# Attention projections as pairs of 64-row matmuls, from the fourth batch on, in a kernel whose order a planner writes

## The chip, the cores and the metric

One core of one Trainium2 chip. The metric is the time of one execution on the device, in microseconds; the kernel before takes 316.47 us, the median of three runs (316.13 to 316.59). Its profiled execution has a span of 314.5 us, with TensorE's granted clock at 1.000.

## What is computed

Attention with random features (Performer), followed by an MLP with a hard-swish gate:

```
q, k, v: (8 batches, 8 heads, 576 tokens, 64); omega: (128 features, 64); fp32
phi(x) = exp(h - max(h)) / sqrt(128),  h = (x s) omega^T - |x s|^2 / 2,  s = 64^-0.25
kv = phi(k)^T v;  z = sum over tokens of phi(k)
attention = phi(q) kv / (phi(q) z + 1e-6)
x = attention as (4608 tokens, 512);  w_in: (512, 2048), w_out: (2048, 512)
h = x w_in;  out = (h * clip(h + 3, 0, 6) / 6) w_out
```

The contraction of the projections `x omega^T` is over the head dimension, 64, half of TensorE's 128 rows.

## The kernel before, in words

**Order.** The kernel doesn't write its instructions in a fixed order. It records its work as operations (`op`, line 86), each with its engine or a choice of engines, an assumed duration, a priority, what it reads and writes, and the PSUM banks that it needs. A list scheduler (`schedule`, line 138) then plays them through on assumed times: of the operations whose inputs are ready it takes the one with the lowest priority number on each engine, and gives out the eight PSUM banks of 128 x 512 fp32 (`ring`) as they come free. `slack` and `dslack` make an operation wait a little longer than its inputs are assumed to take, `spare` asks for so many more free banks than it takes. `emit` writes the result with semaphore waits, so each engine has one fixed queue. The table `NUDGE` (line 20) adds a small number to the priorities of named operations; it was found by a search. No assumed time appears on the chip: a wrong one only gives an order that waits.

**Attention, per batch** (`attention`, line 587). The 576 tokens of 8 heads are 72 chunks of 128 x 64, two side by side in one "double chunk": 18 double chunks. `kT` and `qT` hold them turned, so that the 64 dimensions of the one chunk are on partitions 0 to 63 and those of the other on 64 to 127. For batches 0 to 2 TensorE turns them (L468), from batch 3 on the DMA queues do.
- K (line 676 to 692): for each double chunk, one matmul of all 128 rows with `kT` as weights and `om`, 128 x 256, streaming (L681). `om` is omega transposed twice on the diagonal, with zeros elsewhere, so both chunks come out side by side, in half a PSUM bank; two double chunks fill one bank. ScalarE takes the exponential of a bank (L687), VectorE its maximum by chunk (L690), because the division by the maximum is put off to `v`.
- Q (`project`, line 694): `om[:, lh, :]` as weights, half of whose rows are zero, and up to four double chunks of `qT` streaming, 512 columns; once for lh = 0, once for lh = 1, each into a bank of its own (L698). ScalarE takes the exponential (L702).
- `pair` (line 780), for each two heads: reciprocal of the maxima, `v` scaled by it (L794 on GpSimd or VectorE, L796 on ScalarE), phi(k)^T v and z by L810 and L812, phi(q) times that by L838, and the division by L854.

**MLP, per block of 512 tokens.** `mm1` (line 891): 16 groups of four matmuls of 512 columns (L907), each evacuated by a relu on ScalarE (L913) and a product on VectorE (L915). The second product is done, after the first block, as a seven-product Strassen form (`products`, line 1009, matmuls L1041, sums of tokens on GpSimd L973, sums of results on VectorE L1057). Block b's MLP is recorded beside the attention of batch b + 1, so TensorE's queue is a mixture of both; at the start, while inputs load, fill matmuls (`idle_work`, L505) hold TensorE's clock up.

Of the kernel before, what the change touches and what calls it, by code (L numbers as in the profile page):

```python
# [9 lines left out]
AF = mybir.ActivationFunctionType  # L10
AX = mybir.AxisListType


URGENT = 0.5
FIT = 0.1
IDLE_UNTIL = 21.0
EV0 = (("ACT","DVE"), ("ACT","DVE"), ("POOL","DVE"), {"k": ("POOL", "ACT", "DVE"), "q": ("POOL", "ACT","DVE")})
# [1 line left out]

NUDGE = {  # L20
    ('Tevk0.00', 0): 0.0222, ('Tk0.10', 0): 0.0169, ('Tevk0.10', 0): 0.0216, ('Tk0.11', 0): 0.0313,
    ('Tevk0.11', 0): 0.0172, ('castq0.0A', 0): -0.0176, ('Tq0.1B', 0): -0.0037, ('Tk0.l', 0): 0.0668,
    ('Tevk0.l', 0): -0.1599, ('K0.0', 0): -0.1553, ('eK0.0', 0): -0.0153, ('K0.1', 0): 0.0442,
    ('eK0.1', 0): -0.0653, ('mx0.1', 0): -0.0395, ('eK0.2', 0): -0.042, ('K0.3', 0): 0.0328, ('K0.5', 0): -0.0067,
    ('K0.6', 0): -0.0736, ('eK0.6', 0): 0.0218, ('K0.7', 0): -0.0092, ('eK0.7', 0): 0.0218, ('K0.8', 0): 0.0351,
    ('eK0.8', 0): 0.0218, ('mx0.8', 0): -0.0031, ('kvz.0.0', 0): 0.0057, ('num.0.0A', 0): 0.0042,
    ('rec.0.0A', 0): -0.0049, ('div.0.0A', 0): 0.0356, ('num.0.0B', 0): 0.0126, ('kv.0.1', 0): -0.0134,
    ('num.0.1A', 0): 0.0126, ('rec.0.1A', 0): -0.009, ('Xev.0.1A', 0): 0.0018, ('num.0.1B', 0): -0.0007,
    ('cc.0.2', 0): -0.0088, ('num.0.2A', 0): 0.0126, ('vc.0.3', 0): -0.0114, ('vcc.0.3', 0): -0.0172,
    ('num.0.3A', 0): 0.0126, ('X.0.3B', 0): 0.0821, ('Xev.0.3B', 0): 0.0062, ('numL0', 0): -0.0033,  # L30
    ('divL0', 0): 0.0082, ('divL2', 0): 0.0082, ('k00.1', 0): 0.0095, ('kl.1', 0): -0.0088, ('ql0.1', 0): 0.0145,
    ('vl.1', 0): -0.119, ('v10.1', 0): -0.0099, ('Tevq1.2', 0): 0.0463, ('Tq1.4', 0): 0.0008,
    ('mx1.7', 0): -0.0202, ('mx1.8', 0): 0.0033, ('Q1.0', 1): 0.0073, ('eQ1.0', 1): 0.0199, ('Q1.1', 0): 0.0184,
    ('Q1.1', 1): -0.0218, ('eQ1.1', 1): 0.0077, ('eQ1.2', 1): -0.007, ('vcl.1', 1): -0.0035, ('vc.1.0', 0): 0.0089,
    ('kv.1.0', 0): 0.0071, ('kvz.1.0', 0): -0.0003, ('rec.1.0A', 0): 0.0024, ('div.1.0A', 0): 0.0054,
    ('div.1.0B', 0): 0.0054, ('vc.1.1', 0): 0.0087, ('num.1.1A', 0): -0.002, ('div.1.1A', 0): 0.0054,
    ('div.1.1B', 0): 0.0054, ('Xev.1.1', 0): -0.0002, ('kv.1.2', 0): -0.0042, ('rec.1.2A', 0): -0.0101,
    ('div.1.2A', 0): 0.0075, ('div.1.2B', 0): 0.0054, ('X.1.2', 0): 0.0047, ('rec.1.3A', 0): -0.0016,
    ('div.1.3A', 0): 0.0054, ('div.1.3B', 0): 0.0054, ('mm1.0A.0p', 2): 0.0169, ('mm1.0A.2p', 1): 0.003,
    ('mm1.0A.2p', 2): 0.026, ('mm1.0A.4p', 2): 0.0282, ('mm1.0A.4', 0): 0.0113, ('relu.0A.4', 0): 0.1116,  # L40
    ('mm1.0A.6', 0): -0.0758, ('relu.0A.6', 0): -0.0575, ('mm1.0A.8', 0): -0.0075, ('g.0A.8', 0): -0.037,
    ('g.0A.10', 0): 0.0321, ('relu.0A.12', 0): 0.0317, ('mm1.0A.14', 0): 0.0222, ('relu.0B.12', 0): -0.0169,
    ('k10.2', 0): -0.0002, ('ql0.2', 0): 0.0037, ('K2.5', 0): -0.0042, ('mx2.5', 0): -0.1483, ('K2.7', 0): -0.0504,
    ('K2.8', 0): -0.1148, ('mm2.0.0', 3): -0.0049, ('mm2.0.0', 6): 0.0051, ('mm2.0.1', 2): 0.0111,
    ('mm2.0.1', 5): -0.0042, ('relu.1.7', 0): 0.0128, ('g.1.7', 0): -0.0389, ('g.1.8', 0): 0.0106,
    ('mm2.0.2', 0): -0.0003, ('relu.1.9', 0): 0.0261, ('mm1.1.11', 0): -0.0435, ('mm1.1.12', 0): 0.0488,
    ('k10.3', 0): -0.0369, ('kl.3', 0): 0.0052, ('q00.3', 0): -0.0024, ('q10.3', 0): 0.0694, ('ql0.3', 0): -0.0408,
    ('ql1.3', 0): -0.013, ('kv.3.2', 0): 0.1102, ('kvz.3.3', 0): 0.0243, ('g.2.1', 0): -0.019,
    ('mm2.1.3', 1): 0.0578,
}  # L50


# [24 lines left out]
class Prog:  # L77
# [8 lines left out]
    def op(self, eng, occ, emit, prio, reads=(), writes=(), alloc=(), lat=0.2, group=None, inc=1, name="", slack=0.0, dslack=0.0, issue=0.5, spare=0, packet=46.0):  # L86
        o = Op()
        o.engs = (eng,) if isinstance(eng, str) else tuple(eng)
        o.eng = None
        o.emit, o.occ, o.lat, o.prio, o.name = emit, occ, lat, prio, name  # L90
        o.alloc = list(alloc)
        o.group, o.inc, o.slack, o.dslack, o.issue, o.spare, o.packet = group, inc, slack, dslack, issue, spare, packet
        o.seq = len(self.ops)
        deps = {}
        virts = []
        for kx in reads:
            for d in self.w.get(kx, ()):
                deps[d] = True
            self.r.setdefault(kx, []).append(o)
            if isinstance(kx, Virt):  # L100
                virts.append(kx)
        for kx in writes:
            for d in self.r.get(kx, ()):
                if d is not o:
                    deps.setdefault(d, False)
            for d in self.w.get(kx, ()):
                deps.setdefault(d, False)
            self.w[kx] = [o]
            self.r[kx] = []
            if isinstance(kx, Virt):  # L110
                virts.append(kx)
        for vx in set(virts):
            vx.users.append(o)
            vx.left += 1
        o.virts = list(set(virts))
        o.deps = deps
        o.succ = []
        o.end = o.start = None
        o.emitted = None
        self.ops.append(o)  # L120
        return o
# [231 lines left out]
def _emit(nc, es, q, k, v, omega, w_in, w_out, out):  # L353
    B, H, S, D = q.shape
    M = omega.shape[0]
# [7 lines left out]
    NU = NCH // 4  # L363
# [3 lines left out]
    TU = [(0, 2), (2, 6), (6, 10), (10, 14), (14, 18)]  # L367
# [6 lines left out]
    alpha = float(D) ** -0.25  # L374
# [8 lines left out]
    K0, T0, V0, C0 = EV0  # L383
# [12 lines left out]
    vl = [sbt("vl%d" % u, [128, NP, D + 1], F32) for u in range(2)]  # L396
# [5 lines left out]
    kT = sbt("kT", [128, NDC, 128], BF16)  # L402
    qT = sbt("qT", [128, NDC, 128], BF16)
    qpT = [sbt("qpT", [128, NCH * 128], BF16)] * 2
    kp = [sbt("kp", [128, NCH, M], BF16)] * 2
    mx = [sbt("mx%d" % u, [128, NCH], F32) for u in range(2)]
    cc = [sbt("cc%d" % u, [128, NCH], F32) for u in range(2)]
    vc = [sbt("vc%d" % u, [128, 520], BF16) for u in range(2)]
# [30 lines left out]
    op = G.op  # L439

    def mmt(n):
        return 0.003 + n / 2400.0

    def actt(n):
        return 0.07 + n / 1200.0

    def dvet(n):
        return 0.07 + n / 960.0
# [138 lines left out]
    def attention(b):  # L587
# [80 lines left out]
        else:  # L668
            for t, cst, dst in (("k", KB[pb], kT), ("q", QB[pb], qT)):
                for i, (x0, x1) in enumerate(((0, 10), (10, 18))):  # L670
# [2 lines left out]
                       pos(4.5 * i) - 0.1, reads=rows_of(t, range(x0, x1)),  # L673
                       writes=[(t + "T", x) for x in range(x0, x1)], group="d%sT%d" % (t, i), inc=16,
                       lat=1.0, name="Tdma%s.%d.%d" % (t, b, i), issue=1.2, packet=24.0)
        for u in range(NU):
            vK = Virt(ring)

            def e_K(E, u=u, vK=vK):
                for i in range(2):  # L680
                    ins = E.matmul(ring.t[vK.slot][:, 256 * i:256 * i + 256], kT[:, 2 * u + i, :],  # L681
                                   om[:].rearrange("d t m -> d (t m)"), start=True, stop=True)
                return ins

            op("PE", 2 * mmt(256), e_K, pos(u) + 0.02, reads=[("kT", 2 * u), ("kT", 2 * u + 1)] + omk, writes=[vK],
               alloc=[vK], lat=0.25, slack=sl, dslack=2 * sl, spare=sp, name="K%d.%d" % (b, u))
            op("ACT", actt(512), lambda E, u=u, vK=vK: E.activation(  # L687
                kp[pb][:, 4 * u:4 * u + 4, :].rearrange("p c m -> p (c m)"), ring.t[vK.slot], AF.Exp, scale=alpha),
               pos(u) + 0.02, reads=[vK], writes=[("kp", 0, u)], name="eK%d.%d" % (b, u))
            op("DVE", dvet(512), lambda E, u=u: E.reduce_max(  # L690
                mx[pb][:, 4 * u:4 * u + 4], kp[pb][:, 4 * u:4 * u + 4, :], axis=AX.X),
               pos(u) + 0.03, reads=[("kp", 0, u)], writes=[("mx", pb, u)], name="mx%d.%d" % (b, u))
# [12 lines left out]

        qv = qpT[pb][:].rearrange("m (x l t) -> m x l t", l=2, t=128)
        for i, (d0, d1) in enumerate(TU):
            if i == 0 or b:
                project(str(i), list(range(d0, d1)), qT[:, d0:d1, :],
                        lambda lh, d0=d0, d1=d1: qv[:, d0:d1, lh, :], pos(2 * i) + 0.03 if b else LATE)  # L710
        if b == 0:
# [3 lines left out]
                    project("%d%s" % (m0 // 2, "AB"[s]), every(m0, m1, s), alts(qT, s, m0, m1),  # L715
                            lambda lh, s=s, m0=m0, m1=m1: qa[:, 2 * m0:2 * m1, s, lh, :], 0)
        op("DVE", 0.17, lambda E: E.reciprocal(cc[pb][:, 0:NP], mx[pb][:, 0:NP]), pos(0) + 0.04,
           reads=[("mx", pb, 0)], writes=[("cc", pb, "l")], name="ccl.%d" % b)
        for hh in range(2):
            p0 = 64 * hh  # L720
            op(EV_V if b else V0, {"POOL": 0.72, "DVE": dvet(260)}, lambda E, hh=hh, p0=p0: E.tensor_tensor(
# [58 lines left out]
    def pair(b, m, t):  # L780
# [25 lines left out]
        def e_kv(E):  # L806
# [4 lines left out]
                         start=(i == 0), stop=False)  # L811
            return E.matmul(o[:, 0:130], kp[pb][:, m, :], vcl[pb][:, m, :], start=False, stop=True)  # L812

        op("PE", 8 * 0.03 + 0.06, e_kv, t, reads=[("kp", 0, u) for u in us + [0]] +
           [("vc", u2, i) for i in range(2)] + [("vcl", pb, i) for i in range(2)],
           writes=[vkv], alloc=[vkv], lat=0.25, slack=sl, spare=sp, name="kv" + nm)
        op(EV_K if b else K0, both(130), evac(lambda: kvz[m][:], lambda: ring.t[vkv.slot][:, 0:130]), t, reads=[vkv],
# [405 lines left out]
```

The softmax here doesn't subtract the row's maximum and nothing guards it: scores larger than these inputs give would overflow.

## Time and profile before

| what | time, share or count |
|---|---|
| time, median of 3 | 316.47 us |
| span of the profiled execution | 314.5 us |
| VectorE, GpSimd, ScalarE busy | 74, 72, 64% of the span |
| mm1's matmuls (L907), 512 columns | 512 |
| Strassen products (L1041), 256 columns | 880 |
| K projections (L681), 256 columns | 144 |
| Q projections (L698), 512 or 256 columns | 80 |
| fill matmuls (L505) | 61 |

A row of the page reads: line, engine, operation, what it writes and reads, shapes and how many; then the time in which the engine was busy with them and the mean length of one in ns; then how long the engine sat idle just before them, and which engine's work ended that. TensorE's matmuls overlap in the pipeline and their ends are modelled, so the length of one record (379 ns for 512 columns) is not what it adds to the time; that is read from the starts of successive groups in the timeline.

### The profile page before, as it was taken

The page shows a single profiled execution, that of the slowest core. Times are in us where ns is not written, and L with a number is a line of the kernel's source. Part 1 is how long each engine was busy: PE and PEld are TensorE (multiplying, and loading weights), DVE is VectorE, ACT ScalarE, POOL GpSimd, SP SyncE. Part 2 cuts the span into 40 slices and gives each one's busy share as a digit, 9 for nine tenths or more (in the row PEclk, how much of TensorE's full clock was granted, in tenths as well). Part 3 has the DMA queues.
Part 4 walks back from the last instruction along what each step waited for, and adds up shares of the span by engine and source line. Part 5 has one row for each costly group of instructions (what it writes and reads, how often), then busy time and mean ns, then how long its engine had stood idle before and what let it go on. Part 6 is the DMA issues. An engine that isn't in the chain of part 4 may idle for free.

```text
span 314.5 us, 7018 instructions
## 1 busy us (share of the span) xinstructions
PE 307.1 (98%) x2662; PEld 214.2 (68%) x2662; DVE 233.8 (74%) x511; ACT 200.3 (64%) x465; POOL 227.1 (72%) x247
## 2 busy tenths in 40 slices
PE   8899999999999999999999999999999989999994
PEld 6689956656885688657855785668655954666684
DVE  4979998878799887697399767785879547556533
ACT  3987997899767957863299478842986026343300
POOL 2777253099879987599999896987577819868570
PEclk9999999999999999999999999999999999999999
DMA  8999989554996999099979993999205200300125
GB/s 244 286 202 210 235 133 230 171 67 42 173 216 75 127 257 204 2 127 219 194 161 126 237 186 84 122 240 223 76 15 104 85 9 0 134 2 2 67 85 117
DMA packets 83218, 43.15 MB, mean 137 GB/s; under 512 B 51057, under 2 KB 80881, under 8 KB 83185
## 3 DMA queue, kind: packets, MB, share of 16 engines
q1 hardware_dynamic: 55824, 29.60, 41.0%
q0 software_dynamic: 26576, 12.46, 32.2%
q10 hardware_dynamic: 784, 0.66, 0.7%
q8 instruction: 21, 0.34, 0.5%
q14 instruction: 13, 0.10, 0.1%
HBM read 36.73 MB, written 9.44 MB: 147 GB/s over the span
## 4 chain that ended last, share of the span: by engine, by line
PE 87%; DMA 6%; ACT 2%; DVE 2%; SPq 2%; issue 0%
PE p L907 35%; PE p L1041 31%; DMA v<-in_v_dram 6%; PE p L698 5%; PE p L681 4%; PE p L957 3%; PE p L838 3%; PE p L810 3%; PE p L468 2%; SPq L542 1%; ACT vc L796 1%; ACT kp L687 1%; PE p L932 1%; PE p L1107 1%; PE p L812 1%; DVE mx L690 0%
## 5 line engine op out<-in xcount | busy, mean ns | idle before, releaser
L913 ACT ACTIVATE tsb<-p 128x512 f16<-128x512 f32 x128 | 76.1, 604 | 54.7 <-PE p L907 53.9
L915 DVE SCALAR_TENSOR_TENSOR gT<-tsb,p 128x512 f16<-128x512 f16 x128 | 85.8, 683 | 28.0 <-ACT tsb L913 27.4
L907 PE MATMUL p<-xT,wi 128*128 128x512 bf16 x448 | 106.5, 379 | 0.0
L907 PEld LDWEIGHTS p<-xT,wi 128*128 128x128 bf16 x448 | 42.2, 98 | 42.0
L973 POOL TENSOR_TENSOR s<-gT 128x512 f16<-128x512 f16 x32 | 37.2, 1163 | 22.8 <-DVE gT L915 21.9
L687 ACT ACTIVATE kp<-p 128x512 bf16<-128x512 f32 x72 | 39.0, 611 | 22.5 <-PE p L681 22.5
L690 DVE TENSOR_REDUCE mx<-kp 128x4 f32<-128x512 bf16 x72 | 46.0, 667 | 8.3 <-ACT kp L687 8.3
L1041 PE MATMUL p<-wo,gT 128*128 128x256 f16 x368 | 45.2, 273 | 0.0
L702 ACT ACTIVATE qpT<-p 128x512 bf16<-128x512 f32 (+1 forms) x80 | 41.7, 577 | 1.9 <-PE p L698 1.7
L973 POOL TENSOR_TENSOR gT<-gT,s 128x512 f16<-128x512 f16 x32 | 36.9, 1153 | 6.1 <-PE p L1041 3.7
L1041 PEld LDWEIGHTS p<-wo,gT 128*128 128x128 f16 x368 | 35.8, 98 | 7.7
L973 POOL TENSOR_TENSOR s<-gT,s 128x512 f16<-128x512 f16 x32 | 37.0, 1158 | 4.1 <-DVE gT L915 2.7
L973 POOL TENSOR_TENSOR gT<-gT 128x512 f16<-128x512 f16 x32 | 36.9, 1152 | 2.5
L1041 PE MATMUL p<-t,gT 128*128 128x256 f16 x256 | 32.4, 273 | 0.8 <-DVE u L1057 0.8
L854 DVE TENSOR_TENSOR xb<-p,rec 128x384 bf16<-128x384 f32 (+1 forms) x64 | 28.6, 476 | 0.1
L1041 PEld LDWEIGHTS p<-t,gT 128*128 128x128 f16 x256 | 24.6, 98 | 5.9 <-DVE u L1057 1.1
L796 ACT ACTIVATE vc<-v,cc 128x64 bf16<-128x64 f32 x104 | 26.4, 362 | 1.2 <-DVE cc L788 1.1
L698 PE MATMUL p<-qT,om 128*128 128x512 bf16 (+1 forms) x80 | 24.4, 358 | 0.1
L794 POOL TENSOR_TENSOR vc<-v,cc 128x512 bf16<-128x512 f32 x17 | 17.8, 1045 | 8.4 <-DVE cc L788 6.2
L681 PE MATMUL p<-om,kT 128*128 128x256 bf16 x144 | 22.0, 274 | 0.0
L542 POOL DMA_DIRECT2D k<-in_k_dram x12 | 9.4, 786 | 16.4 <-PE p L907 15.5
L1057 DVE TENSOR_TENSOR u<-p 128x512 f32<-128x512 f32 x16 | 11.0, 688 | 12.3 <-PE p L1041 12.3
(94 smaller groups left out, 438.3 us busy)
## 6 DMA issues: line engine op xcount, KB each, us to landing
v<-in_v_dram SPq DMA_DIRECT2D x14, 512.0 KB, 7.1
out_dram<-osb SPq DMA_DIRECT2D x14, 512.0 KB, 3.7
wi<-in_moe_w_in_dram POOLq DMA_DIRECT2D x4, 512.0 KB, 9.3
k<-in_k_dram POOLq DMA_DIRECT2D x8, 256.0 KB, 4.7
k<-in_q_dram POOLq DMA_DIRECT2D x8, 256.0 KB, 7.0
wo<-in_moe_w_out_dram POOLq DMA_DIRECT2D x8, 256.0 KB, 11.3
kb<-in_k_dram POOLq DMA_DIRECT2D x6, 256.0 KB, 4.6
qb<-in_q_dram POOLq DMA_DIRECT2D x6, 256.0 KB, 6.8
```

The source lines that it names most:

```text
L681: ins = E.matmul(ring.t[vK.slot][:, 256 * i:256 * i + 256], kT[:, 2 * u + i, :], om[:].rearrange("d t m -> d (t m)"), start=True, stop=True)
L687: op("ACT", actt(512), lambda E, u=u, vK=vK: E.activation(kp[pb][:, 4 * u:4 * u + 4, :].rearrange("p c m -> p (c m)"), ring.t[vK.slot], AF ...
L690: op("DVE", dvet(512), lambda E, u=u: E.reduce_max(mx[pb][:, 4 * u:4 * u + 4], kp[pb][:, 4 * u:4 * u + 4, :], axis=AX.X), pos(u) + 0.03, r ...
L698: op("PE", mmt(n), lambda E, vQ=vQ, lh=lh: E.matmul(ring.t[vQ.slot][:, 0:n], om[:, lh, :], src, start=True, stop=True), p + 0.045 * lh, re ...
L702: op("ACT", actt(n), lambda E, vQ=vQ, lh=lh: E.activation(dst(lh), ring.t[vQ.slot][:, 0:n].rearrange("m (j t) -> m j t", t=128), AF.Exp, s ...
L796: ins = E.activation(vcm[:, i, 0:D], v32[:, m, i, :], AF.Copy, scale=cc[pb][:, c0 + i:c0 + i + 1])
L854: op("DVE", dvet(128 * n), lambda E: E.tensor_tensor(xv(i0, i1), psum()[:, :, :, 0:64], rbc, ALU.mult), t + 0.01, reads=[vn, ("rec", ru)], ...
L907: ins = E.matmul(ring.t[vh.slot], wi[:, c, 128 * f:128 * f + 128], xv[:, c, :], start=(c == 0), stop=(c == NJ - 1))
L913: op("ACT", actt(512), lambda E: E.activation(tsb[tu][:], ring.t[vh.slot], AF.Relu, bias=0.5, scale=1.0 / 6.0), t - 0.1, reads=[vh], write ...
L915: op("DVE", dvet(512), lambda E: E.scalar_tensor_tensor(gT[gu][:, f, :], tsb[tu][:], 1.0, ring.t[vh.slot], ALU.min, ALU.mult), t - 0.1, re ...
L973: op(engines, {"POOL": 0.05 + n / 490.0, "DVE": 0.07 + n / 1920.0}, lambda E: E.tensor_tensor(dst, x, y, ALU.subtract if minus else ALU.ad ...
L1041: ins = E.matmul(ring.t[v.slot][:, 256 * j:256 * j + 256], a[:, f, 128 * j:128 * j + 128], w[:, f, :], start=(first and f == 0 and j == 0) ...
```

## The change

From batch 3 on (`ROWS = 3`), K and Q of a range of double chunks are projected together by one operation on TensorE, `project_rows`. Each matmul uses only the 64 rows that hold its chunk: partitions 0 to 63 for the one, 64 to 127 for the other, with the matching half of `om`, so no product with zeros is left, and the two can run side by side in the two halves of the array. A range of four double chunks takes four banks at once (K and Q, each for both halves), the first range of two takes two banks. There are five such bursts in a batch. For K there are now twice as many matmuls, of 128 columns instead of 256. The planner counts such a burst as 0.22 us (`SWITCH`) plus the time of two full-width streams of its length. The exponentials and maxima are taken by half instead of by double chunk, with a step over the other half in what they write. The leftover tokens' keys get names of their own (`kpl`, `mxl`), so that the operations that need them depend on their burst alone.

The table `NUDGE` is replaced: many more entries, and larger ones (before up to 0.16, after up to 3.3), so that operations of the whole kernel, batches 0 to 2 and the MLP too, stand in another order and in part on another engine. TensorE's list has 59 fill matmuls instead of 61, and ScalarE's has 72 scalings of 64 elements (`vc`) instead of 104, GpSimd's 22 of 512 elements instead of 17.

```diff
+SWITCH = 0.22
+ROWS = 3
...
 NUDGE = {
...
-        for u in range(NU):
+        def project_rows(i, d0, d1):
+            n = d1 - d0
+            u = max(2 * i - 1, 0)
+            vs = [Virt(ring) for _ in range(2 if n == 2 else 4)]
+            def bank(w, lh):
+                c = 128 * n * w if n == 2 else 0
+                return vs[lh if n == 2 else 2 * w + lh], c
+            def out_of(w, lh):
+                vx, c = bank(w, lh)
+                return ring.t[vx.slot][:, c:c + 128 * n]
+            def e(E):
+                for x in range(n):
+                    for lh in range(2):
+                        E.matmul(out_of(0, lh)[:, 128 * x:128 * x + 128], kT[64 * lh:64 * lh + 64, d0 + x, :],
+                                 om[64 * lh:64 * lh + 64, lh, :], start=True, stop=True)
+                for lh in range(2):
+                    ins = E.matmul(out_of(1, lh), om[64 * lh:64 * lh + 64, lh, :],
+                                   qT[64 * lh:64 * lh + 64, d0:d1, :], start=True, stop=True)
+                return ins
+            op("PE", SWITCH + 2 * mmt(128 * n), e, pos(u) + 0.02,
+               reads=[(t + "T", x) for t in "kq" for x in range(d0, d1)] + omk, writes=vs, alloc=vs, lat=0.25,
+               slack=sl, dslack=2 * sl, spare=0, name="R%d.%d" % (b, i))
...
+        if b >= ROWS:
+            for i, (d0, d1) in enumerate(TU):
+                project_rows(i, d0, d1)
+        for u in range(NU if b < ROWS else 0):
...
-            if i == 0 or b:
+            if b < ROWS and (i == 0 or b):
                 project(str(i), list(range(d0, d1)), qT[:, d0:d1, :],
```

## The prediction

> **What bounds the kernel now.** I read the page's busy line, its forty slices and the chain first, then TensorE's own waits, then the timeline of TensorE in one steady stretch, because a busy TensorE need not be a full one.
>
> ```profile
> PE 307.1 (98%) x2662; PEld 214.2 (68%) x2662; DVE 233.8 (74%) x511; ACT 200.3 (64%) x465; POOL 227.1 (72%) x247
> PE   8899999999999999999999999999999989999994
> ...
> PE 87%; DMA 6%; ACT 2%; DVE 2%; SPq 2%; issue 0%
> ...
> L681 PE MATMUL p<-om,kT 128*128 128x256 bf16 x144 | 22.0, 274 | 0.0
> ```
>
> No other engine is over 74%, and the chain is 87% TensorE. All of TensorE's idle time that has a cause is in three single waits (columns: total us, times, longest us):
>
> ```profile
> PE p L505 <- DVE fill L500: 1.3, 1, 1.3
> PE p L810 <- DVE vcl L721: 0.9, 1, 0.9
> PE p L1041 <- DVE u L1057: 0.8, 1, 0.8
> ```
>
> The first two lie before 16 us. The timeline (start, us, group) then says whether the busy time is dense:
>
> ```profile
> 157.73 0.60 PE L681 MATMUL p<-om,kT 128*128 128x256 bf16 x4
> 158.17 4.48 PE L907 MATMUL p<-xT,wi 128*128 128x512 bf16 x20
> 162.49 0.60 PE L698 MATMUL p<-qT,om 128*128 128x256 bf16 x3
> 162.92 1.03 PE L907 MATMUL p<-xT,wi 128*128 128x512 bf16 x4
> 163.78 0.38 PE L698 MATMUL p<-qT,om 128*128 128x512 bf16 x1
> 164.00 0.42 PE L810 MATMUL p<-vc,kp 128*128 128x65 bf16 x8
> 164.26 0.22 PE L812 MATMUL p<-vcl,kp 128*128 128x130 bf16 x1
> ```
>
> Start to start, 20 matmuls of 512 columns take 162.49-158.17 = 4.32 us, 0.216 each; four of 256 take 0.44, 0.109 each; eight of 65, each with a weight load of its own, take 0.26, 0.033 each. That is one column per cycle at 2.4 GHz plus some 2 ns, with no pause between groups: the stream is full. From about 20 us to the last matmul near 310 us the time is the sum of these pitches, so what leaves TensorE's stream leaves the span, unless a new wait appears.
>
> **What the Trainium skill says.** "TensorEngine Tiling (Array Packing)", Key Properties: two 64-row tiles can load weights and multiply in parallel, and changing the tiling mode, not just the tile, drains TensorE. "TensorE: Matmul & The Clock Gate", Part 3, The mechanism: a weight load overlaps a running matmul of another row group, and two matmuls of different row groups start some 4 ns apart. The trace of before has only 128-row matmuls (every form reads 128*128), so it shows neither the pairing nor the drain. The first page's Gotcha 1: PSUM Pressure adds that concurrent row tiles need different PSUM banks; the new code gives the two halves of a pair different banks.
>
> **The change part by part.** (1) Removed, batches 3 to 7: 18 K matmuls of 256 columns per batch (L681, half of whose products are with the zero half of `om`), 18 x 0.109 = 1.96 us, and eight Q matmuls of 512 and two of 256 (L698), 8 x 0.216 + 2 x 0.109 = 1.95 us. Five batches: 5 x 3.91 = 19.5 us of the full stream.
>
> (2) Added: 36 K matmuls of 128 columns and the same ten Q matmuls per batch, all 64 rows high, so in pairs. K: 90 pairs in all. One matmul of 128 columns streams in 0.056 (the transposes' pitch, 16 in 0.89 us in the chain), but a pair carries two weight loads, and two matmuls with a load each go no faster than 2 x 0.030 to 2 x 0.033 (L838, L810 at 65 columns). I take 0.063: 90 x 0.063 = 5.7 us. Q: a pair takes one pitch, 20 x 0.216 + 5 x 0.109 = 4.9 us. Sum 10.6, so 8.9 us saved before switching.
>
> (3) Switches. The 25 bursts stand at 23 places in TensorE's new order (two places hold two bursts), so the array goes over and back 46 times. Nothing in the trace is like it. From below: the array has to empty its 128 rows, about the 0.056 us of one 128-column stream, an estimate. From above: the whole latency that a matmul's record has beyond its pitch, 0.379-0.216 = 0.163 us, plus a weight load that can no longer hide, 0.098 (L681's load rows): 0.26 us. I take 0.11, nearer the lower end, because fetching operands can go on while the array empties; that it can is assumed. The planner books 0.22 per burst, the same figure, but it is no measurement here. 46 x 0.11 = 5.1 us (2.6 to 12.0). Net of (1) to (3): -3.8 us.
>
> (4) ScalarE and VectorE. The exponentials read the same elements; five bursts give 10 K exponentials and 10 maxima per batch instead of 9 and 9. Some 0.2 us per batch and engine, hidden: in the sums by stretch the two are busy 24.5 and 26.6 of the 32 us from 158 to 190. Over the whole kernel the new order takes 32 of ScalarE's 64-element scalings (four `vc` groups) and one of VectorE's `vc` away and gives GpSimd five more of about 1 us. GpSimd is the fullest of the three, 28.9 of those 32 us, still behind TensorE, and its sums feed products that stand well behind them in TensorE's order.
>
> (5) A new wait. A burst of four chunks needs four free PSUM banks of eight before its first matmul, and all TensorE work behind it stands in the same queue. ScalarE empties a bank in about 0.49 us (three exponentials in 1.47 us in the chain). One late bank costs at most about that; the planner places bursts where it expects four to be free, and for 128 single banks of L907 the trace shows no idle time. I allow 0.4 us in all; if half of the 25 waited for one bank, it would be 6 us.
>
> (6) The other priorities. The only wait of the steady part is this one, where the product that reads `t` needs a bank whose sum VectorE has yet to take:
>
> ```profile
> 251.80 1.91 PE L1041 MATMUL p<-wo,s 128*128 128x256 f16 x16
> 254.50 1.05 PE L1041 MATMUL p<-t,gT 128*128 128x256 f16 x8 [0.79 <-DVE u L1057]
> ```
>
> Sixteen matmuls from 251.80 end their stream at 253.55, so 0.95 us are lost. In the new order mm1 groups stand between these two, 2.6 us of work, which covers the wait: -0.8 us. At the head TensorE runs fill matmuls (L505) until about 20 us; there are 59 instead of 61 before the stream is full, 2 x 0.109 = -0.2 us. The final products and stores stay in place: zero.
>
> Sum: -3.8 +0.4 -0.8 -0.2 = -4.4, so 316.5-4.4 = 312.1; I give 312.0.
>
> **The rivals.** Cheap switches: at 0.056 each they cost 2.6 us, and the sum becomes -8.9+2.6-1.0+0.4 = -6.9, 309.6 us. For it: operands are fetched ahead in the stream today. Dear switches: at 0.26 they cost 12.0 us, -8.9+12.0-0.6 = +2.5, 319.0 us, slower than before; for it, the weight load and the fetch sit in line after a drain; against it, fetch and drain would have to exclude each other wholly. Bank waits: half the bursts wait 0.49 us, +6 us on -4.8, 317.7 us; for it, mm1's PSUM rows and the bursts share eight banks and one ScalarE; against it, no such idle time in the trace now. No pairing: if the two halves run one after the other, the streams are 180 x 0.056 + 40 x 0.216 + 10 x 0.109 = 19.8 us against 19.5, and with switches and the rest the sum is +4.8, 321.3 us; the skill's page speaks against it.
>
> **How the numbers follow.** Likeliest case 0.58, cheap switches 0.24, dear switches (0.2 and more) 0.08, bank waits 0.06, no pairing 0.04. The middle ground between my switch price and the dear one crosses no change at 0.2 us a switch: (8.9+0.6)/46. So within 0.2% (315.8 to 317.1) 0.05, faster 0.81, slower 0.14. The range has to take in the cheap end, 309.6 less a us for K pairs at 0.056 and a better head, and most of the way to no change: 308.5 to 315.8.
>
> **What would show it.** New rows for 64-row matmuls, 180 of 128 columns and 50 for Q, with a lone burst of four chunks taking, with its switches, about 4 x 0.063 + 0.216 + 2 x 0.11 = 0.69 us, where its work took 4 x 0.109 + 2 x 0.216 = 0.87 before. Two matmuls of one pair should start within tens of ns. The gap in front of a burst's first matmul and behind its last gives the price of a switch directly. TensorE's waits should show no releaser ScalarE of more than a few tenths, and the 0.8 us on `u` should be gone. The forecast is wrong if a burst takes over 0.87 us, if K pairs start 0.11 apart, or if the head before 20 us has moved by over 1 us.

## The result, and the profile after

The changed kernel takes 313.02 us (median of six, 310.89 to 313.37) against 316.61 us (316.13 to 317.96) for the kernel before beside it: a ratio of 0.987 [0.984, 0.990]. Two later sets of runs of both kernels gave 311.94 us, 0.986 [0.984, 0.989], and 311.64 us, 0.985 [0.982, 0.988]. So the change is worth 1.3 to 1.5%, 3.6 to 4.7 us by the medians; 312.0 was predicted.

From the page of the changed kernel, in the order in which the page of before was read: the busy line, TensorE's forty slices, and the chain by engine.

```profile
PE 301.0 (97%) x2723; PEld 204.4 (66%) x2750; DVE 231.9 (74%) x511; ACT 195.5 (63%) x448; POOL 230.2 (74%) x246
PE   7999999999999999999999999998999999999993
...
PE 80%; POOL 8%; ACT 3%; DMA 2%; issue 2%; DVE 2%; SPq 1%; POOLq 0%; DVEq 0%
```

TensorE still sets the time. As forecast, the other engines stay behind it: VectorE stays at 74%, ScalarE loses a point, GpSimd gains two. But GpSimd has gone from nothing to 8% of the chain, and TensorE's waits name it (columns: total us, times, longest us):

```profile
PE p L548 <- DVE fill L543: 1.3, 1, 1.3
PE p L1132 <- POOL s L1064: 0.8, 1, 0.8
PE p L511 <- POOL kb L500: 0.8, 1, 0.8
```

The first is the old wait for the fill operand. Of before's other two, on `vcl` and `u`, neither is left; a wait on GpSimd's sum `s` and one on GpSimd's conversion of `k` have come. None names ScalarE, and in the second profile of this kernel (the first experiment) each lone burst of four took 0.64 us to within 2 ns, so no such burst waited for a bank. Line numbers are shifted: L1041 of before is L1132, L681 and L698 are L736 and L739 where bursts replace them.

The timeline of TensorE in the changed kernel shows bursts between second products (start, us, group):

```profile
183.18 1.04 PE L1132 MATMUL p<-wo,gT 128*128 128x256 f16 x8
184.15 0.40 PE L736 MATMUL p<-om,kT 64*128 64x128 bf16 x8
184.38 0.38 PE L739 MATMUL p<-qT,om 64*128 64x512 bf16 x2
184.70 1.92 PE L1132 MATMUL p<-wo,s 128*128 128x256 f16 x16
186.45 1.04 PE L1132 MATMUL p<-t,gT 128*128 128x256 f16 x8
```

Eight products from 183.18 end their stream at 183.18 + 8 x 0.109 = 184.05. The next stream starts at 184.70, so the burst of four double chunks took 0.64 us with both its switches; 0.87 was its price before, 0.69 was predicted. (A batch has 18 double chunks, which are 36 chunks and not 72 as the description has it; hence its 36 K matmuls.) From the starts of the single matmuls: 0.096 us pass before the first. Four K pairs follow, the two of a pair 3 to 4 ns apart, the second pair 0.067 us after the first, the others 0.056. Then comes the Q pair, and 0.092 us more than Q's 0.216 pass until the next 128-row matmul. The matmul after that one is late once more, 0.120 us behind it instead of 0.109. So on both sides of a burst a change of mode shows in two places: as a gap of 0.092 to 0.096 us, and as some 0.010 us by which what follows the first matmuls of the new mode is late. Both are there at all 23 places of the second profile; together they are 0.104 us a switch.

**Where the time went.** The same sums from the starts in each trace: the head (first start, fill matmuls and waits up to 25 us), later waits, K and Q of batches 3 to 7 with their switches, and the tail from the end of the last matmul's stream (its start and its pitch). What is left, 276.1 us, is the same stream in all but for 0.3 us. Where there are bursts, the later waits hold the late matmul behind each of them, 23 x 0.010 = 0.2 us, which is a cost of switching.

| us | before | after | after, again | full rows | new priorities only | switch twice | fills and sums |
|---|---|---|---|---|---|---|---|
| head | 12.4 | 13.3 | 12.3 | 11.6 | 11.9 | 11.6 | 11.6 |
| second half of `k` landed at | 6.1 | 7.4 | 6.8 | 6.1 | 6.2 | 6.0 | 6.1 |
| later waits | 2.0 | 2.2 | 2.3 | 1.4 | 1.8 | 2.4 | 2.0 |
| K and Q, batches 3 to 7 | 19.5 | 14.7 | 14.7 | 19.8 | 19.5 | 20.6 | 14.7 |
| tail | 4.4 | 5.1 | 5.3 | 5.0 | 4.4 | 4.4 | 4.4 |
| span | 314.5 | 311.4 | 310.6 | 313.8 | 314.0 | 315.1 | 308.9 |

(The last five columns are experiments below; after's trace lacks the records of 27 matmuls, which are counted by their pitch.) After against before: -4.8 for the projections, +0.9 for the head, +0.2 for later waits (the late matmuls behind the bursts), +0.7 for the tail, together -3.0, as the spans say (-3.0). Three questions follow: are the pairs really what pays, and at what price of a switch; what did the new priorities do; and what are the head and the tail.

**The head.** GpSimd's conversion of `k`, of before and then of after (start, us, group, and in brackets the idle time ahead of it):

```profile
6.14 0.61 POOL L457 CAST kb<-k 128x512 bf16<-128x512 f32 x1 [1.71 <-DMA k<-in_k_dram]
```

```profile
7.48 0.61 POOL L500 CAST kb<-k 128x512 bf16<-128x512 f32 x1 [3.25 <-DMA k<-in_k_dram]
```

The second half of `k` was issued at 1.66 us in both, and landed 1.3 us later in the one trace. In the other traces of kernels with this head it landed at 6.0 to 7.6 us, and the head's length follows it. This is scatter of the transfers at the start, not of the change. Where `k` landed by 6.2, the head of the new order measured 11.6 to 11.9, under before's 12.4, but that isn't shown to be the order's doing, as the one profile of before doesn't stand for its own order. An experiment below (pairs with the old priorities) has the same 838 matmuls in the same order until 88 us, with `k` landing at 6.26, and its last fill matmul starts 0.86 us earlier. Here is that matmul of before and then of that run:

```profile
20.17 0.27 PE L505 MATMUL p<-fill 128*128 128x256 bf16 x1
```

```profile
19.31 0.27 PE L507 MATMUL p<-fill 128*128 128x256 bf16 x1
```

In before, eight transposes from 5.24 us took 0.85 us and a wait at 15 us took 0.94; in that run they took 0.48 and 0.59. One profile of a head is good to about a microsecond, whatever the order.

**The tail.** SyncE's stores at the end, of before and then of after (start, us for the whole group of issues):

```profile
304.01 6.49 SPq L1133 DMA_DIRECT2D out_dram<-osb  x6
310.60 2.08 SPq L1119 DMA_DIRECT2D out_dram<-osb  x3
```

```profile
302.62 5.10 SPq L1224 DMA_DIRECT2D out_dram<-osb  x6
307.82 1.84 SPq L1210 DMA_DIRECT2D out_dram<-osb  x3
```

Before, the six issues are stretched over 6.49 us because they wait for products. In the new order they stand close together, and one of them, at 305.51, took 1.56 us instead of 0.6. The DMA queues of after from 302.6 to 308 us (packets, MB, share of 16 engines) have a stranger among the stores:

```profile
q1 hardware_dynamic: 627, 0.58, 50.1%
q10 hardware_dynamic: 80, 0.07, 5.4%
q8 instruction: 1, 0.02, 1.5%
```

One packet of 16 KB of instructions is 1.5% of 16 engines x 5.4 us = 1.3 us on one DMA engine. It started at 305.39. That it is what lengthens the issue was only a guess at this point.

### The profile page after: what moved, and what is told of

Its sections match the earlier page's. It is cut to its first block, busy times and chain, and to the rows that moved or that the text cites. A ratio compares the mean times of both kernels' runs of the same rounds, so it can differ in the third digit from the quotient of the medians.

```text
span 311.4 us, 7144 instructions
## 1 busy us (share of the span) xinstructions
PE 301.0 (97%) x2723; PEld 204.4 (66%) x2750; DVE 231.9 (74%) x511; ACT 195.5 (63%) x448; POOL 230.2 (74%) x246
## 4 chain that ended last, share of the span: by engine, by line
PE 80%; POOL 8%; ACT 3%; DMA 2%; issue 2%; DVE 2%; SPq 1%; POOLq 0%; DVEq 0%
PE p L998 30%; PE p L1132 27%; PE p L1048 5%; PE p L1023 4%; POOL s L1064 4%; PE p L929 2%; DMA q<-in_q_dram 2%; PE p L511 2%; PE p L900 2%; PE p L736 2%; POOL gT L1064 1%; POOL vc L884 1%; PE p L739 1%; PE p L771 1%; PE p L788 1%
## 5 line engine op out<-in xcount | busy, mean ns | idle before, releaser
L1004 ACT ACTIVATE tsb<-p 128x512 f16<-128x512 f32 x128 | 74.8, 600 | 45.1 <-PE p L998 36.7
L998 PE MATMUL p<-xT,wi 128*128 128x512 bf16 x427 | 101.2, 379 | 1.5 <-issue 0.3
L1132 PE MATMUL p<-wo,gT 128*128 128x256 f16 x368 | 45.7, 273 | 0.0
L1064 POOL TENSOR_TENSOR s<-gT 128x512 f16<-128x512 f16 x32 | 37.0, 1156 | 11.8 <-DVE gT L1006 9.8
L1132 PEld LDWEIGHTS p<-wo,gT 128*128 128x128 f16 x368 | 35.0, 98 | 6.8 <-issue 0.8
L749 ACT ACTIVATE kp<-p 128x512 bf16<-128x512 f32 (+1 forms) x50 | 25.8, 560 | 19.4 <-PE p L739 19.3
L754 DVE TENSOR_REDUCE mx<-kp 128x4 f32<-128x512 bf16 (+1 forms) x50 | 29.6, 625 | 4.5 <-ACT kp L749 4.0
L1132 PE MATMUL p<-t,gT 128*128 128x256 f16 x256 | 32.1, 273 | 0.0
L884 POOL TENSOR_TENSOR vc<-v,cc 128x512 bf16<-128x512 f32 x22 | 23.4, 1062 | 6.9 <-DVE cc L878 4.9
L758 ACT ACTIVATE qpT<-p 128x512 bf16<-128x512 f32 (+1 forms) x50 | 26.5, 576 | 2.2 <-PE p L739 2.2
L1132 PEld LDWEIGHTS p<-t,gT 128*128 128x128 f16 x256 | 24.2, 98 | 5.6 <-issue 1.2
L1148 DVE TENSOR_TENSOR u<-p 128x512 f32<-128x512 f32 x16 | 11.0, 690 | 13.4 <-PE p L1132 13.4
L780 DVE TENSOR_REDUCE mx<-kp 128x4 f32<-128x512 bf16 x27 | 17.5, 675 | 1.2 <-ACT kp L777 1.2
L886 ACT ACTIVATE vc<-v,cc 128x64 bf16<-128x64 f32 x72 | 18.2, 351 | 0.0
L811 POOL TENSOR_TENSOR vcl<-vl,cc 64x260 bf16<-64x260 f32 x14 | 8.7, 620 | 11.8 <-DVE cc L807 11.0
L929 PEld LDWEIGHTS p<-kvz,qpT 128*128 128x128 bf16 x312 | 14.2, 98 | 4.9 <-ACT qpT L792 0.5
## 6 DMA issues: line engine op xcount, KB each, us to landing
wo<-in_moe_w_out_dram POOLq DMA_DIRECT2D x8, 256.0 KB, 12.3
```

The lines of the kernel that those rows point to most:

```text
L749: op("ACT", actt(128 * n), lambda E, lh=lh, ko=ko: E.activation(ko, out_of(0, lh).rearrange("p (x m) -> p x m", m=M), AF.Exp, scale=alpha) ...
L754: op("DVE", dvet(128 * n), lambda E, ko=ko, mo=mo: E.reduce_max(mo, ko, axis=AX.X), pos(u) + 0.03, reads=[("kp", 0, u + lh) if i else ("kp ...
L758: op("ACT", actt(128 * n), lambda E, lh=lh: E.activation(qd[:, d0:d1, lh, :], out_of(1, lh).rearrange("m (j t) -> m j t", t=128), AF.Exp, ...
L884: return E.tensor_tensor(vcm[:, :, 0:D], v32[:, m, :, :], cbc, ALU.mult)
L886: ins = E.activation(vcm[:, i, 0:D], v32[:, m, i, :], AF.Copy, scale=cc[pb][:, c0 + i:c0 + i + 1])
L929: ins = E.matmul(d[:, hh, i - i0, :], qpT[pb][:, o:o + 128], kvz[m][:, 65 * hh:65 * hh + 65], start=True, stop=True)
```

## The experiments

**The changed kernel again**, to know what repeats. No edit.

> The changed kernel once more. By its first profile the 25 bursts put 14.7 us on TensorE where 19.5 stood, 4.8 us saved, but the span fell by 3.0: about 0.9 us went at the head, where the second half of k, whose transfer is issued at 1.66 us in both kernels, landed at 7.43 instead of 6.09 us, and 0.7 us at the tail, where SyncE issued the last stores 1 us after their data. Theory A (chance of the transfers): in this profile the landing is earlier or later with no change of the code, and span and landing move together; with the landing at 6.1 the span is 309 to 310. Theory B (the new order makes it so): landing at 7.4 and tail 5.1 us again, span 311.4 within 0.3.

Measured: 311.94 us (311.13 to 312.73), ratio 0.986 [0.984, 0.989], span 310.6. The bursts (14.7), the wait near 214 (1.0) and the long tail (5.3, a store issue of 1.74 us) are there again; the head is 1.1 shorter with `k` landing 0.6 earlier. So the length of the head is chance; the other three are there in both profiles.

**Bursts with all 128 rows**: the changed kernel's order and bursts, but each matmul takes the zero half with it, so nothing runs side by side and the array is never switched.

```diff
-    E.matmul(out_of(0, lh)[...], kT[64 * lh:64 * lh + 64, d0 + x, :], om[64 * lh:64 * lh + 64, lh, :], ...)
+    E.matmul(out_of(0, lh)[...], kT[:, d0 + x, :], om[:, lh, :], ...)
...
-    ins = E.matmul(out_of(1, lh), om[64 * lh:64 * lh + 64, lh, :], qT[64 * lh:64 * lh + 64, d0:d1, :], ...)
+    ins = E.matmul(out_of(1, lh), om[:, lh, :], qT[:, d0:d1, :], ...)
```

> The same order of all queues, but each matmul of a burst uses all 128 rows, with the zero half of om: nothing can pair, no mode switch. Theory A (the pairs save, the switches cost 0.094 us each): a burst of four chunks takes 8 x 0.056 + 2 x 0.216 = 0.88 us instead of 0.642 with its switches, one of two 0.44 instead of 0.42; 20 x 0.24 + 5 x 0.02, and about 0.2 less where two bursts share their switches: +5 us on the changed kernel, 318 us. Rival (the gain is in the new order alone, and pairs only make up for their switches): within 1 us of the changed kernel.

Measured: 316.04 us (315.22 to 317.38), ratio 1.000 [0.998, 1.002]: the whole gain is gone. TensorE's timeline of this kernel, the same burst:

```profile
184.15 1.04 PE L1132 MATMUL p<-wo,gT 128*128 128x256 f16 x8
185.02 0.61 PE L736 MATMUL p<-om,kT 128*128 128x128 bf16 x8
185.47 0.59 PE L739 MATMUL p<-qT,om 128*128 128x512 bf16 x2
185.90 1.91 PE L1132 MATMUL p<-wo,s 128*128 128x256 f16 x16
```

Without a switch the burst starts as the stream ends (184.15 + 0.87 = 185.02), and it takes 185.90 - 185.02 = 0.88 us instead of 0.64. Over 25 bursts that is 19.8 against 14.7 us. The medians differ by 4.1 us rather than 5.1 (from the changed kernel's 311.94). The profiles name what may have gone the other way: without switches no matmul behind a burst is late, 0.2 us, the wait on GpSimd is 0.5 us shorter here, the tail 0.3 and the head 0.7.

**Pairs with the old priorities, and new priorities without pairs**: the two halves of the change, each alone.

```diff
-NUDGE = { ... the new table ... }
+NUDGE = { ... the table of before ... }
```

> The pairs and bursts with the table of priorities of the kernel before. Theory A (the saving is TensorE's own, whatever the order): 311 to 313 us. Rival (a burst needs four banks at once, and with the old priorities several bursts of a batch come late and back to back, with the products that need their exponentials directly behind, so TensorE waits for ScalarE): slower than the kernel before, by 5 us or more, and TensorE's waits name ScalarE and VectorE.

```diff
-ROWS = 3
+ROWS = 99
```

> The table of priorities of the changed kernel, but all batches projected as before (ROWS beyond the last batch), so every TensorE instruction of the kernel before is there, and the new entries for the bursts meet no operation. Theory A (the new order is worth about nothing by itself: its one covered wait of 0.95 us is paid back): 315.5 to 317.5. Rival (the order brings a part of the gain): 314 or less.

Measured: pairs with the old table 331.02 us (median of three, 330.96 to 331.49; a fourth execution took 337.36), ratio 1.048 [1.044, 1.051]; the new table without pairs 316.09 us (315.35 to 317.5), ratio 1.000 [0.998, 1.001]. TensorE's waits of the first:

```profile
PE p L957 <- DMA xT<-xb: 4.0, 1, 4.0
PE p L1091 <- POOL s L1023: 2.7, 3, 1.3
PE p L1091 <- DVE u L1107: 2.0, 3, 0.8
PE p L695 <- ACT qpT L717: 1.6, 3, 0.7
```

With those of the view that are not shown, and without the fill's, they are 16.1 us, spread over every releaser, with one block's activations landing 4 us late. Behind that long wait, from 271.7 to 275.1 us, the granted clock was 0.50, and the matmuls of 512 columns came at half their pace; keeping the clock from that is what the fill matmuls at the start are for. In the second, TensorE's timeline has one wait in place of before's 0.79 on `u`:

```profile
224.08 1.05 PE L1132 MATMUL p<-t,gT 128*128 128x256 f16 x8 [0.47 <-DVE u L1148]
```

So the new priorities have no gain of their own: as far as these waits tell, their part is to give the bursts, and the work around them, places where inputs and banks are ready. The two halves alone give 0 and +15 us, together -4. The saving can't be split between them by adding.

**Each burst switched twice as often**: one more 128-row matmul of 64 columns between K and Q of each burst, its product overwritten by Q's.

```diff
+    E.matmul(out_of(1, 0)[:, 0:64], ident[:], fill[:, 0:64], start=True, stop=True)
     for lh in range(2):
         ins = E.matmul(out_of(1, lh), om[64 * lh:64 * lh + 64, lh, :], ...)
```

> The changed kernel with one full-height matmul of 64 columns put between the K and the Q matmuls of each of the 25 bursts, its result overwritten by Q: two more mode switches per burst, all queues else as they were. Theory A (each switch costs the 0.094 us that stands before and behind a burst in the trace): a burst of four takes 0.642 + 0.188 + 0.03 = 0.86 us, and the kernel 25 x 0.22 = 5.4 us more, 317.5. Rival (those gaps are waits for PSUM banks or semaphores at the ends of a burst, and switching is cheap): 25 x 0.03, less than 1 us more.

Measured: 316.27 us (315.83 to 317.63), ratio 1.001 [1.000, 1.003]. TensorE's timeline:

```profile
185.64 1.04 PE L1133 MATMUL p<-wo,gT 128*128 128x256 f16 x8
186.61 0.40 PE L736 MATMUL p<-om,kT 64*128 64x128 bf16 x8
186.94 0.20 PE L738 MATMUL p<-fill,ident 128*128 128x64 bf16 x1
187.08 0.39 PE L740 MATMUL p<-qT,om 64*128 64x512 bf16 x2
187.40 1.92 PE L1133 MATMUL p<-wo,s 128*128 128x256 f16 x16
```

From the end of the stream ahead (185.64 + 0.87 = 186.51) to the next is 0.89 us instead of 0.64. The 64 columns are some 0.03 us of that (half of the 128-column pitch of 0.056), the two extra switches the rest, 0.1 each. In the sum by trace the bursts cost 20.6 instead of 14.7 us, 5.9 / 25 = 0.235 each, 0.10 per switch, as the gaps and late matmuls of the changed kernel had it (0.104). The median rose by less, 4.3 us from 311.94; against that profile, the head is 0.7 us shorter here and the tail 0.9. A switch has a price that doubling doubles; the rival that switches cost next to nothing, and that pairs run short of their ideal for another reason, falls.

This trace held something unlooked for: its tail is 4.4 us, as before. The 25 extra matmuls had moved the packet of instructions from 2.8 us behind the first late store to 1.7 us ahead of it.

**Three of the late stores on ScalarE's queue**: if SyncE's queue of issues is what makes the tail long, half of it elsewhere shortens it; if the packet holds up a DMA engine, it doesn't matter who issues.

```diff
-op("ACT" if blk == 8 and p0 and c0 and not i else "SP", ...
+op("ACT" if blk == 8 and p0 else "SP", ...
```

> The changed kernel with three of the last block's half stores issued by ScalarE, idle by then, instead of SyncE; nothing else moves. Theory A (the longer tail is SyncE's queue: the fetch of instructions holds one DMA engine for 1.3 us amid six stores, one issue takes 1.6 us instead of 0.6, and the last stores are issued 1 us after their data): the time from TensorE's last matmul to the end falls from 5.1 or 5.2 to about 4.3 us, time 0.9 us less. Rival (the stores' transfers, not their issue, are the limit): tail within 0.2 us, same time.

Measured: 312.02 us (311.4 to 312.9), ratio 0.988 [0.986, 0.991]; tail 5.0. The packet started at 306.4, and now it was an issue of ScalarE, at 305.94, that took 1.77 us instead of 0.6. The theory of SyncE's queue falls.

**GpSimd's two sums swapped.** The wait of the changed kernel near 214 us, in TensorE's timeline:

```profile
213.88 1.04 PE L1132 MATMUL p<-wo,gT 128*128 128x256 f16 x8
215.74 1.05 PE L1132 MATMUL p<-t,s 128*128 128x256 f16 x8 [0.82 <-POOL s L1064]
```

213.88 + 0.87 = 214.75, so 0.99 us are lost. GpSimd works on a sum for a later product (S15.2) ahead of the one that this product needs (S25.3); the edit moves only the latter ahead of the former.

```diff
 G.schedule()
+at = {o.name: i for i, o in enumerate(G.order) if o.name in ("S15.2", "S25.3")}
+late = G.order.pop(at["S25.3"])
+G.order.insert(at["S15.2"], late)
```

> The changed kernel with two neighbours in GpSimd's queue of the sixth MLP block swapped: the sum that TensorE waits for at 214 us goes ahead of one that is needed later. Theory A (TensorE's one long wait of the steady part, 1.0 us, is GpSimd's order at this place): the wait shrinks to 0.1 us or less and the span by 0.9 us. Rival (GpSimd is full there, and TensorE meets the next late sum or bank a few us later): the wait goes but others take its place, span within 0.3 us.

Measured: 311.1 us (310.59 to 313.64), ratio 0.986 [0.983, 0.989]. TensorE's timeline at that place:

```profile
213.23 1.04 PE L1132 MATMUL p<-wo,gT 128*128 128x256 f16 x8
214.10 1.04 PE L1132 MATMUL p<-t,s 128*128 128x256 f16 x8
```

The wait is gone without a new one: later waits fall from 2.3 to 1.4 us. In the time the gain isn't shown: the median is 0.84 us lower than that of the changed kernel run again, but the kernel before was 0.3 lower beside it too, and the ratios, 0.986 and 0.986, do not differ. So it was the order of two operations on GpSimd, and not GpSimd's load, that made TensorE wait.

**Fill matmuls as halves**: each of the 59 fills as two of 128 columns, 59 more matmuls for the same columns, which moves every later fetch of TensorE's instructions.

```diff
-E.matmul(ring.t[vw.slot][:, 0:256], fill[:, 0:128], fill[:, 128:384], ...)
+for h in range(2):
+    ins = E.matmul(ring.t[vw.slot][:, 128 * h:128 * h + 128], fill[:, 0:128],
+                   fill[:, 128 + 128 * h:256 + 128 * h], ...)
```

> The changed kernel with each of the 59 fill matmuls of the head, 256 columns, made as two of 128: the same time on TensorE, but 118 more instructions (a weight load goes with each matmul) ahead of everything else, so the fetches of instructions for TensorE come earlier by half the distance between two. Theory A (the tail is long because such a fetch, 16 KB on one DMA engine for 1.3 us, falls 2.8 us behind the first of the last stores, while in kernels with a tail of 4.36 us it falls ahead of them or beside the first): the fetch at 305.4 moves ahead of the stores and the tail is 4.4 us, span and time 0.7 to 0.8 us less. Rival (the tail comes from the stores' own closeness, whatever the fetch): tail 5.0 or more.

Measured: 312.42 us (311.73 to 315.62), ratio 0.989 [0.985, 0.993]. The packet went to 298.9 us, ahead of the first late store at 303.31, and the tail to 4.39, as expected. The span did not follow, because this profile has a longer wait than the others near 41 us, where `v` landed at 40.6 us instead of 37.5 to 39.7 (TensorE's waits):

```profile
PE p L793 <- ACT kp L782: 1.7, 1, 1.7
```

So the place of the packet makes the tail long: this run and the one with doubled switches moved it ahead of the stores, and both have the short tail. Its worth in the time is not shown.

**Both, fills as halves and sums swapped.** The edits are the two above.

> Both small changes together, the halved fill matmuls and the two swapped sums of GpSimd. If each does what its own run shows in the trace (0.9 us of wait, 0.7 us of tail), the span is 1.6 us under the changed kernel's, about 308.8, time 310.3; if the steady part is full elsewhere, only the tail's part is left, 311.2.

Measured: 310.74 us (310.21 to 311.65), ratio 0.983 [0.980, 0.987], span 308.9. SyncE's stores, and the queues from 300.7 to 306 us:

```profile
300.75 4.14 SPq L1229 DMA_DIRECT2D out_dram<-osb  x6
```

```profile
q1 hardware_dynamic: 755, 0.69, 61.1%
q10 hardware_dynamic: 80, 0.07, 4.8%
```

No packet of instructions, six issues in 4.14 us instead of 5.10, tail 4.36, no wait near 214.

**The changed kernel and this version side by side.** No new edit.

> The changed kernel once more, to stand beside the next run on the same chip. If its two earlier comparisons hold: ratio 0.987 to the kernel before, about 312.0 us; a wait of about 1 us on GpSimd's sum near 214 us, the fetch of TensorE's instructions about 2.9 us behind the first late store, and a tail of about 5.1 us.

> Fills as halves and the two sums of GpSimd swapped, beside the changed kernel on the same chip. If the wait on GpSimd's sum (1.0 us) and the late fetch (0.7 us) are both real costs: about 1.3 to 1.7 us less than the run beside it, tail 4.4 us, no wait near 214. Rival: the gain of the earlier comparison was chance of the transfers at the start; then within 0.5 us of the run beside it.

Measured: the changed kernel 311.64 us (311.3 to 312.15), ratio 0.985 [0.982, 0.988]; with both edits 311.44 us (310.27 to 311.79), ratio 0.983 [0.980, 0.986]. The difference of 0.2 us is far below what was expected. In the two profiles the later waits are 2.38 and 1.33 us; the 1.0 us near 214 is there in the first and gone in the second. The tails are 4.56 and 4.38 us: in this run of the changed kernel the packet fell at 304.7, still among the stores, yet lengthened only one issue to 1.03 us, so its harm is 0.2 to 0.9 us from run to run. What took the rest back is the head, GpSimd's timeline of the changed kernel and then of the version with both edits:

```profile
6.39 0.61 POOL L500 CAST kb<-k 128x512 bf16<-128x512 f32 x1 [2.11 <-DMA k<-in_k_dram]
```

```profile
7.65 0.61 POOL L500 CAST kb<-k 128x512 bf16<-128x512 f32 x1 [3.42 <-DMA k<-in_k_dram]
```

The heads are 11.8 and 13.4 us. Both edits remove what they were to remove, but that the version with both is faster than the changed kernel was not shown: its ratios to before are the lowest of all, and overlap those of the changed kernel. Whether halved fills make a late `k` likelier is open; in the runs with them it landed at 6.1, 6.5 and 7.6, without them at 6.0 to 7.4.

## Why the prediction was right, point by point

| step | predicted, us | measured, us |
|---|---|---|
| (1) removed stream | -19.5 | -19.5 |
| (2) and (3) pairs and switches | +15.7 | +14.9 (14.7, and 0.2 in the late matmuls behind the bursts) |
| (4) ScalarE, VectorE | 0 | no wait on either over 0.2 in the steady part of the first profile |
| (5) waits for banks | +0.4 | 0: each lone burst of four took 0.64 |
| (6) other waits | -0.8 | 0.0 |
| (6) head | -0.2 | +0.9 in the profile; open, within the scatter |
| (6) tail | 0 | +0.7 in the profile; +0.2 to +0.9 |
| sum | -4.4 | -3.0 (spans); -3.6 to -4.7 (medians) |

**The pairs** were right in kind, and each size a little too dear. The two matmuls of a pair start 3 to 4 ns apart, as the Trainium skill says in "TensorE: Matmul & The Clock Gate", Part 3, The mechanism. A K pair takes 0.056 us, the pitch of one matmul; the prediction's 0.063, from the pitch of two matmuls with a weight load each, counted a load that in fact hides, 90 x 0.007 = 0.6 us too much. A switch costs 0.104 us, a gap of 0.094 and 0.010 behind it, not 0.11: 46 x 0.006 = 0.3 us too much. Against that stand 0.2 us, two short waits on VectorE's `u` behind the two places with two bursts. The Trainium skill says in "TensorEngine Tiling (Array Packing)", Key Properties, that changing the tiling mode drains TensorE. The runs show a cost at every change, as that would have it, with a price that the page doesn't give: above the stream of 128 columns (0.056), well under the prediction's upper end (0.26). What the array does in that time they don't show, so that the price came out near the 0.11, which was a choice between those two ends, is partly luck. The rivals of dear switches and no pairing fall by the single burst (0.64 us), that of cheap switches by the doubled switch, that of bank waits by the list of waits.

**The priorities** are where the prediction's reading was too narrow. Step (6) looked only at the wait that the new order covers. That 0.95 us did go, and half a us near 45 us with it in the first profiles, though five later ones, one of them of the changed kernel itself, have waits of 0.4 to 2.1 us near 41 us; but a search over the whole order makes new neighbours, and one of them put TensorE 0.99 us behind GpSimd. The prediction named GpSimd the fullest engine and passed on because "its sums feed products that stand well behind them": true on the average, false at one place in 310 us, and the swap of two sums showed it in the trace. The runs with one half of the change alone add what the prediction didn't ask at all: without its new order the pairing costs 15 us.

**"The final products and stores stay in place: zero"** failed as well. TensorE's products end 4.4 us before the end in both orders, but the six stores stand closer together, and so a fetch of instructions, whose place depends on how many instructions lie ahead, can hit them with nothing behind which to hide. It was there before, too (a store issue of 1.37 us at 304.75), but SyncE then waited for products until 307.51 in any case. In the new order the tail was 4.36 to 4.39 us in the five profiles where the packet lay ahead of the stores, and 4.56 to 5.25 in the six where it lay among them; with the old order (pairs with the old priorities) it lay among them and the tail was 4.38.

**The head**: 0.2 us can be neither confirmed nor refuted here. In the first profile `k` landed 1.3 us late, and the head was 0.9 us longer, close to the 1 us that the prediction had named as a sign of being wrong; but before's own head differs by 0.9 us from the same order in another run. That the sum came so near is in part luck, because the misses cancel: the pairs and switches cost 0.8 us less than was put down and the banks 0.4 less, against 0.8 more for the other waits and 0.2 to 0.9 for the tail.

## What to carry to other kernels

Where a contraction fills half of TensorE's rows, two halves side by side save nearly half of its stream, but the trips to the 64-row mode and back must be paid for: at 0.104 us a trip, a burst of four double chunks saved 0.22 us of 0.87, and the burst of two (0.42 us from the starts and 0.01 behind it, against 0.44 before) next to nothing. Such a burst wants several free banks at once, so the order of the other engines has to be made anew around it; price both together, since here each alone was worth nothing or less. After any reordering, look for the one wait that was not there before, rather than at the averages, and compare more than one profile before a microsecond at the start is believed.

## What the runs showed that had not been expected

- A fetch of TensorE's instructions is a packet of 16 KB that holds one DMA engine for 0.9 to 1.3 us near the end of these runs. Among the stores it stretched one store's issue from 0.6 to between 1.03 and 1.77 us, on whichever queue that was, and the stores ahead of it landed late: two, issued at 304.01 and 304.67, took 3.9 and 3.5 us against 2.4 in the version without the packet. That it is TensorE's is inferred: only instructions of TensorE were added where it moved.
- Adding instructions can shorten a tail: with 25 or 59 more matmuls that packet lay ahead of the stores.
- The second half of `k`, issued at the same time, landed anywhere from 6.0 to 7.6 us. In the new order the head grew with it from 11.6 to 13.4 us, against 3.6 to 4.7 us for the whole change.
- The first matmuls after a change between 128-row and 64-row mode are followed some 0.010 us late, besides the gap of 0.094 us ahead of them. Measured between two gaps alone, a switch looks a tenth too cheap.
